# Selective attention and a gelu MLP on one core: narrow fills at the begin, none ahead of two attention steps, two items by halves, and DMA transposes moved between stores

## The chip, the cores and the metric

The kernel runs on one core of one Trainium2 chip. The metric is the device time of one execution in microseconds; before the change it is 306.07 us, the median of three runs (305.69 to 306.65).

## What is computed

There are 8 batches of 8 heads with 576 positions and 64 dimensions a head. Scores get a causal mask and a decay from the running sum of `s`, then a softmax; the result, with the heads side by side, is `x` with 4608 rows of 512. Two matrix products with an exact gelu between them follow.

```
scores = scale * np.matmul(q, k.transpose(0, 1, 3, 2))
bias = -(cum[:, :, :, None] - cum[:, :, None, :])          # cum: running sum of max(s, 0)
scores = np.where(causal, -1000000000.0, scores + np.minimum(bias, 0.0))
attn = softmax(scores)
x = (attn @ v) with heads side by side                     # 4608 x 512
out = gelu(x @ w_in) @ w_out                               # 512 -> 2048 -> 512
```

## The kernel before, in words

The work is cut in 9 chunks of 512 rows of `x`. While chunk `c` goes through the two products of the MLP, the attention of the next batch is computed between them, and the tensors of the batch after that are loaded. All of it is written out in order by hand (a manual schedule): each engine executes its instructions in the order of the program, and the eight PSUM banks are given out by name: three pairs of banks X, Y and Z and two single ones, M[0] and M[1]. `bank(slot, ...)` (L97) hands a slot on, and whoever writes it next waits until those who used it last are done.

Batch 0 has nothing in front of it, so its attention stands alone at the begin of the program, before the loop over the chunks:

- `fill` (L399) issues matrix products of ones whose result nobody reads. There are 28 of 192 columns at the begin, into M[1], then pairs of 512 columns at six places, one behind the first transposes and five between the later steps of batch 0.
- `tr_mm` and copies bring q and k of batch 0 into `qkT[0]` (q and k with positions along the free dimension). The first transposes wait for the load of `fq`.
- `sc_first(p, u, slot)` (L446) does the scores of one pair of heads in two parts: products of `off_bf` first, which put the mask into the bank (L453, L459), then those of q and k (L465), then one exponential on ScalarE (L471). The third and fourth pair (p = 2, 3) need the second half of the heads, whose k is copied last (L397 on VectorE).
- `av_first` (L542) sums the exponentials, weighted: the denominators into `d_ps`, the outputs into `oo`. It is done for the first 256 rows (part 0, banks M[0] and X) and for the next 256 (part 1, the second sums: banks M[1] and Y).
- `x_first` (L548) makes 1/denominator on ScalarE as exp(-ln) (L510, L511), and VectorE multiplies it into `xT` (L552), for one half of the heads at a time. So there are four ln, four exp and four products, in one order on each engine.
- `l1_first` (L578) is the hidden layer for items 0 and 1 of chunk 0, in quarters: first for the first 256 rows with the first half of the contraction (`k0 = 0`), items 0 and 1, then with the second half, then the same for the next 256 rows. Item 0 uses bank Z, item 1 bank X.

An item of the hidden layer is 256 of its 2048 columns: eight products of 512 columns in one pair of banks (`l1_item`, L595, products L605), then a gelu on ScalarE. Item `f2` uses the bank pair `f2 % 3` of the chunk's order, so item 7 takes over the bank of item 4. `layer1` (L798) issues items 2 to 7 one after another.

The batches from 2 on bring q and k in another way. POOL loads token rows (`load_tok`, L172) into buffers `tok`, one for each of the five stretches of 128 positions (the last has 64), and SP issues a DMA transpose for each into `qkT` (`transpose_tok`, L187, L190). SP's queue is in order. It also has the stores of chunk 0's four results (`l2_out`, L636) and loads of v for later batches (L204). Before the change the five transposes of batch 2 are issued at the begin of chunk 1, behind all stores of chunk 0, and POOL's loads of batch 3's tokens wait for them, as they use the same buffers. The scores of batch 2 (L436) come behind the hidden layer of chunk 1.

Of the kernel before, what the change touches and what calls it, by code (L numbers as in the profile page):

```python
# [19 lines left out]
def kernel(  # L20
# [22 lines left out]
    ST = 5  # L43
# [53 lines left out]
    def bank(slot, shape, dtype, name):  # L97

        return ps.tile(shape, dtype, tag=slot, bufs=1, name=name)
# [84 lines left out]
                    ),  # L184
                )

    def transpose_tok(b):  # L187
        for st in range(ST):
            n_st = 128 if st < ST - 1 else SL
            nc.sync.dma_start_transpose(  # L190
                out=qkT[b % 2][:, :, :, st * 128 : st * 128 + n_st].rearrange("d i p t -> d (i p) t"),
                in_=tok_of.pop((b, st))[:n_st].rearrange("t i c -> t (i c)"),
            )
# [19 lines left out]
    def absmax(b, ps_=range(NP)):  # L213

        for p in ps_:
            nc.vector.tensor_reduce(  # L216
                amx[:, b * NP + p], qkT[b % 2][:, :, p, :S], axis=AX, op=ALU.max, apply_absolute_value=True
            )

    def square_x(c):  # L220

        junk = work.tile([128, NP, NB], bf16, tag="junk", bufs=1, name="junk")
        nc.scalar.activation(  # L223
            junk, xT[:, :, c * NB % XW : c * NB % XW + NB], func=AF.Square, accum_out=sqx[:, c : c + 1]
        )

    def scale_v(b, sts, eng):

        t = raws[b, "v"].rearrange("p st h (d t) -> p st h t d", t=2)
        vb = vv[b % 2].rearrange("p st h (t d) -> p st h t d", t=2)  # L230
        for st0, st1 in sts:
            n_st = 128 if st1 < ST else SL
            for st in range(st0, st1):
                eng.tensor_tensor(  # L234
                    vb[:n_st, st], t[:n_st, st],
                    wb[:n_st, st, b * H : b * H + H].unsqueeze(2).unsqueeze(3).to_broadcast([n_st, H, 2, D // 2]),
                    op=MULT,
                )
# [154 lines left out]
    def copy(eng, out, in_):  # L393
        if eng is nc.scalar:
            eng.copy(out, in_)  # L395
        else:
            eng.tensor_copy(out, in_)  # L397

    def fill(t, n):  # L399

        cols = t.shape[1]
        for _ in range(n):
            nc.tensor.matmul(  # L403
                t, lhsT=xT[:, 3, 1024:1152], rhs=xT[:, 3, 1024 : 1024 + cols],
                start=True, stop=True, skip_group_check=True,
            )
# [21 lines left out]
    def sc_mm(b, p, slots, u0=0):  # L428
        if u0 == 0:
            P_of[b, p] = work.tile([128, 2, PW], bf16, tag="P", bufs=4, name="P")  # L430
        P = P_of[b, p]
        for u, slot in enumerate(slots, u0):
            s_ps = bank(slot, [128, 2, 512], fp32, "sc_ps")
            for jt, i0, n, off in UNITS[u]:
                for e in range(2):
                    nc.tensor.matmul(  # L436
                        s_ps[:, e, off : off + n],
                        lhsT=qkT[b % 2][e * 64 : e * 64 + 64, 1, p, jt * 128 : jt * 128 + 128],
                        rhs=qkT[b % 2][e * 64 : e * 64 + 64, 0, p, i0 : i0 + n],
                        start=True, stop=True,  # L440
                    )
            nc.scalar.activation(  # L442
                P[:, :, UO[u] : UO[u] + UW[u]], s_ps[:, :, : UW[u]], func=AF.Exp, scale=scale
            )
# [30 lines left out]
    def mask(b, p, eng):  # L475
        P = P_of[b, p]
        for u in range(NU):
            d = P[:, :, UO[u] : UO[u] + 512].rearrange("p e (g c) -> p e g c", c=256)[:, :, :, 0:128]
            eng.tensor_tensor(  # L479
                d, d, tri_bf.unsqueeze(1).unsqueeze(1).to_broadcast([128, 2, 2, 128]), op=MULT  # L480
            )
            if u == 1:
                d = P[:, :, UO[u] + 448 : UO[u] + 512]
                eng.tensor_tensor(
                    d, d, tri_bf[:, :64].unsqueeze(1).to_broadcast([128, 2, 64]), op=MULT
                )
# [55 lines left out]
    def av_first(c, qds, d_ps, oo, what=(None, 0, 1)):  # L542

        for qd in qds:
            for t in what:
                av_mm(0, qd, d_ps[:, qd] if t is None else oo[:, qd, t], t, PART[c])
# [48 lines left out]
    def l1_item(c, f2, k0=0, k1=None):  # L595
        k1 = KO if k1 is None else k1
        if f2 == 0 and k0 == 0:
            gT_of[c] = work.tile([128, FT, NB], fp16, tag="gT", bufs=1, name="gT")
        if k0 == 0:
            h_of[c, f2] = bank(order[c][f2 % 3], [128, 2, NB], fp32, "h_ps")  # L600
        h_ps = h_of[c, f2]
        for i in range(2):
            ft = f2 * 2 + i
            for ko in range(k0, k1):
                nc.tensor.matmul(  # L605
                    h_ps[:, i, :], lhsT=w_in_r[:, ko, ft * 128 : (ft + 1) * 128],
                    rhs=xT[:, ko, c * NB % XW : c * NB % XW + NB],
                    start=(ko == 0), stop=(ko == KO - 1),
                )
        if k1 == KO and f2 < FT // 2 - 1:  # L610
            nc.scalar.activation(gT_of[c][:, f2 * 2 : f2 * 2 + 2, :], h_ps, func=AF.Gelu)  # L611
        elif k1 == KO:
            for i in range(2):
                nc.scalar.activation(gT_of[c][:, f2 * 2 + i, :], h_ps[:, i], func=AF.Gelu)  # L614

    def l2_item(c, sub, f0=0, f1=FT, slot=None, eng=None, later=False):

        gT = gT_of[c]
        if f0 == 0:
            if slot is None:  # L620
                o_of[c, sub] = bank(M[sub % 2], [128, KO * 128], fp32, "o_ps")
            elif slot in M:
                o_of[c, sub] = bank(slot, [128, KO * 128], fp32, "o_ps")
            elif sub == 2:
                two = bank(slot, [128, 2, KO * 128], fp32, "o_ps")
                o_of[c, 2], o_of[c, 3] = two[:, 0], two[:, 1]
        o_ps = o_of[c, sub]
        for ft in range(f0, f1):
            nc.tensor.matmul(  # L629
                o_ps, lhsT=gT[:, ft, sub * 128 : (sub + 1) * 128],  # L630
                rhs=w_out_r[:, ft], start=(ft == 0), stop=(ft == FT - 1),
            )
        if f1 == FT and not later:
            l2_out(c, sub, eng)

    def l2_out(c, sub, eng=None):  # L636

        o_sb = work.tile([128, KO * 128], fp32, tag="osb", bufs=4, name="o_sb")
        copy(eng or nc.vector, o_sb, o_of[c, sub])
        r0 = c * NB + sub * 128  # L640
        nc.sync.dma_start(out=out[r0 : r0 + 128], in_=o_sb)
# [85 lines left out]
        load_w(1, i)  # L727
    both = (nc.vector, nc.vector)
    f_ps = bank(M[1], [128, 512], fp32, "fill")
    fill(f_ps[:, :192], 28)  # L730
    t_q = bank(X, [128, 2, 16, 64], bf16, "tr_ps")
    tr_mm(0, 0, 0, [t_q[:, pp] for pp in range(2)])
    nc.scalar.copy(
# [31 lines left out]
                t_k[:, pp, :FR, j * 32 : j * 32 + 32].rearrange("d r t -> d t r"),  # L765
            )
    f_ps = bank(M[1], [128, 512], fp32, "fill")
    fill(f_ps, 2)
    sc_first(2, 0, Y)
    fill(f_ps, 2)  # L770
    sc_first(3, 0, Z)
# [8 lines left out]
    oo0 = bank(X, [128, 2, 2, 256], fp32, "av_o")  # L780
    av_first(0, (0, 1), d0, None, (None,))
    av_first(0, (0, 1), None, oo0, (0, 1))
    fill(f_ps, 2)
    d1 = bank(M[1], [128, 2, 256], fp32, "av_d")
    av_first(1, (0, 1), d1, None, (None,))
    for qd in range(2):
# [11 lines left out]
    def layer1(c, after):  # L798

        for k0, k1 in ((0, KO - 2), (KO - 2, KO)):  # L800
            for f2 in range(2):
                if c > 0:
                    l1_item(c, f2, k0, k1)
            if c == 1 and k0 == 0:
                av_tails(1, M[0])
        after(1)
        for f2 in range(2, HT):
            l1_item(c, f2)
            after(f2)

    def products(c, order_):
# [4 lines left out]
    for c in range(NCH):  # L816
# [36 lines left out]
                    cert_4(M[1])  # L853

        if c == 1:
            transpose_tok(2)
            load_tok(3)
            absmax(1, [2, 3])
        elif c > 1:
            if nb < B:  # L860
                transpose_tok(nb)
                if nb + 1 < B:
                    load_v(nb + 1, nc.sync)
                    load_tok(nb + 1)
                scale_v(nb, STS[0:3], nc.vector)
            if c < B:
                square_x(c - 1)
                absmax(c, [0, 1])
        layer1(c, after)
        if c == 0:  # L870
            exp_set()
# [21 lines left out]
            l2_item(c, 2, 8, 12)  # L893
            l2_item(c, 3, 8, 12)
            sc_mm(1, 2, (z, x))
            l2_item(c, 0, 12, eng=nc.scalar)
            weight_sums(2)
            sc_mm(1, 3, (z,))
            l2_item(c, 1, 12, later=True)
            sc_mm(1, 3, (x,), 1)  # L900
            l2_out(c, 1, nc.scalar)
            scale_v(1, STS[0:2], nc.vector)
            mask(1, 2, nc.vector)
            scale_v(1, STS[2:5], nc.vector)
            l2_item(c, 2, 12, eng=nc.scalar)
            mask(1, 3, nc.vector)
            av_main(1, 0, M[0], z)
            l2_item(c, 3, 12)
# [263 lines left out]
```

## Time and profile before

| | |
|---|---|
| median of three runs | 306.07 us (305.69 to 306.65) |
| the profiled execution | 305.94 us |
| its span | 304.2 us |
| TensorE (PE) busy | 294.3 us, 97% |
| VectorE (DVE) busy | 226.1 us, 74% |
| ScalarE (ACT) busy | 225.2 us, 74% |
| mean granted TensorE clock | 0.997 |

A profile is one execution. Times are microseconds from the begin of the span. PE is TensorE's matrix products, PEld its weight loads, SPq and POOLq are the DMA queues of SP and POOL. In a row of the timeline the first number is the start, the second the time from there to the end of the last of its instructions, "xN" their count, and the bracket tells how long the engine sat idle before it and who ended that. "issue" is time in which the engine waited for nothing that the profile shows. PE's products are pipelined: the busy time of one is longer than the step to the next, so the pitch is read from starts. A few per cent of the product records are missing, so that counts can be one or two short. A row of a tile or line has the shortest, median and longest duration in ns, then the first and last start.

### The profile page before, as it was taken

The page shows a single profiled execution, that of the slowest core. Times are in us where ns is not written, and L with a number is a line of the kernel's source. Part 1 is how long each engine was busy: PE and PEld are TensorE (multiplying, and loading weights), DVE is VectorE, ACT ScalarE, POOL GpSimd, SP SyncE. Part 2 cuts the span into 40 slices and gives each one's busy share as a digit, 9 for nine tenths or more (in the row PEclk, how much of TensorE's full clock was granted, in tenths as well). Part 3 has the DMA queues.
Part 4 walks back from the last instruction along what each step waited for, and adds up shares of the span by engine and source line. Part 5 has one row for each costly group of instructions (what it writes and reads, how often), then busy time and mean ns, then how long its engine had stood idle before and what let it go on. Part 6 is the DMA issues. An engine that isn't in the chain of part 4 may idle for free.

```text
span 304.2 us, 8151 instructions
## 1 busy us (share of the span) xinstructions
PE 294.3 (97%) x3391; PEld 192.9 (63%) x3412; DVE 226.1 (74%) x511; ACT 225.2 (74%) x291; POOL 79.6 (26%) x103
## 2 busy tenths in 40 slices
PE   7989999999999999999999999999999999999993
PEld 6565444546884588458945785488547864884583
DVE  5758278976897878996997699768977874563751
ACT  3898757778797788878877987798788889575500
POOL 8883447446005500451027101720000000000000
PEclk9999999999999999999999999999999999999998
DMA  7999999999959993899399957997640220031004
GB/s 120 228 211 207 205 228 147 285 172 137 158 135 177 156 172 96 164 151 170 101 159 179 162 112 166 148 157 139 141 84 2 71 71 1 2 103 34 3 1 148
DMA packets 124748, 40.33 MB, mean 133 GB/s; under 512 B 109440, under 2 KB 122752, under 8 KB 124704
## 3 DMA queue, kind: packets, MB, share of 16 engines
q0 software_dynamic: 63280, 17.18, 57.1%
q1 hardware_dynamic: 61136, 22.31, 38.1%
q8 instruction: 28, 0.46, 0.7%
q10 hardware_dynamic: 288, 0.26, 0.3%
q14 instruction: 16, 0.13, 0.2%
HBM read 36.85 MB, written 9.44 MB: 152 GB/s over the span
## 4 chain that ended last, share of the span: by engine, by line
PE 89%; ACT 3%; DMA 3%; POOL 1%; issue 1%; DVE 1%; SPq 1%; ACTq 0%; POOLq 0%
PE h_ps L605 37%; PE pb L682 14%; PE pa L682 8%; PE pd L682 5%; PE pe L682 5%; PE sc_ps L436 4%; PE av_o L495 4%; PE o_ps L629 4%; DMA qkT<-tok 3%; PE av_d L495 1%; ACT P L442 1%; PE h_ps L587 1%; PE av_t L495 1%; PE tr_ps L388 1%; PE fill L403 1%
## 5 line engine op out<-in xcount | busy, mean ns | idle before, releaser
L605 PE MATMUL h_ps<-xT,w_in_r 128*128 128x512 bf16 x542 | 121.9, 379 | 1.1
L605 PEld LDWEIGHTS <-w_in_r 128*128 128x128 bf16 x560 | 54.5, 98 | 63.8 <-DVE xT L532 0.4
L611 ACT ACTIVATE gT<-h_ps 128x1024 f16<-128x1024 f32 x61 | 60.5, 1022 | 28.1 <-PE h_ps L605 28.1
L442 ACT ACTIVATE P<-sc_ps 128x1024 bf16<-128x1024 f32 x56 | 53.7, 1024 | 8.9 <-PE sc_ps L436 8.8
L682 PEld LDWEIGHTS <-gs 128*128 128x128 f16 x512 | 48.6, 98 | 7.5 <-issue 1.3
L178 POOL DMA_DIRECT2D tok<-in_q_dram x30 | 25.6, 852 | 104.2 <-DMA qkT<-tok 101.5
L664 DVE TENSOR_TENSOR gs<-gT 128x512 f16<-128x512 f16 (+1 forms) x80 | 29.1, 365 | 23.6 <-ACT gT L611 20.4
L216 DVE TENSOR_REDUCE amx<-qkT 128x2 f32<-128x1152 bf16 x32 | 42.2, 1343 | 0.1
L682 PEld LDWEIGHTS <-gT 128*128 128x128 f16 x384 | 37.0, 98 | 6.7 <-ACT gT L614 0.2
L682 PE MATMUL pa<-w_out_r,gT 128*128 128x256 f16 x256 | 31.6, 273 | 0.0
L682 PE MATMUL pb<-w_sums,gs 128*128 128x256 f16 x256 | 30.7, 273 | 0.0
L479 DVE TENSOR_TENSOR P<-P,tri_bf 128x512 bf16<-128x512 bf16 x56 | 22.3, 421 | 9.9 <-ACT P L442 9.8
L178 POOL DMA_DIRECT2D tok<-in_k_dram x30 | 25.8, 861 | 3.8 <-DMA w_out_r<-in_moe_w_out_dram 2.3
L234 DVE TENSOR_TENSOR vv<-raw_v,wb 128x512 bf16<-128x512 f32 (+1 forms) x40 | 25.4, 682 | 0.0
L532 DVE TENSOR_TENSOR xT<-av_o,ln 128x256 bf16<-128x256 f32 (+2 forms) x64 | 21.4, 385 | 3.4 <-ACT ln L511 2.5
L223 ACT ACTIVATE junk<-xT 128x2048 bf16<-128x2048 bf16 x9 | 17.1, 1898 | 0.1
L511 ACT ACTIVATE ln<-ln,lnb 128x256 f32<-128x256 f32 x32 | 16.3, 508 | 1.0
L436 PE MATMUL sc_ps<-qkT 64*128 64x256 bf16 x280 | 16.5, 250 | 0.5 <-DMA qkT<-tok 0.5
L664 DVE TENSOR_TENSOR gs<-gs,gT 128x512 f16<-128x512 f16 (+1 forms) x40 | 14.9, 372 | 1.4
L495 PE MATMUL av_o<-P,vv 128*32 128x256 bf16 (+1 forms) x528 | 15.3, 256 | 0.6 <-issue 0.6
L629 PE MATMUL o_ps<-w_out_r,gT 128*128 128x512 f16 x64 | 15.5, 380 | 0.2 <-ACT o_sb L395 0.2
L495 PEld LDWEIGHTS <-vv 128*32 128x32 bf16 x784 | 15.0, 96 | 1.1 <-issue 0.7
(131 smaller groups left out, 328.6 us busy)
## 6 DMA issues: line engine op xcount, KB each, us to landing
out_dram<-o_sb SPq DMA_DIRECT2D x35, 256.0 KB, 2.5
raw_v<-in_v_dram SPq DMA_DIRECT2D x20, 256.0 KB, 10.1
raw_v<-in_v_dram POOLq DMA_DIRECT2D x12, 256.0 KB, 6.7
tok<-in_q_dram POOLq DMA_DIRECT2D x24, 128.0 KB, 7.5
tok<-in_k_dram POOLq DMA_DIRECT2D x24, 128.0 KB, 8.1
w_out_r<-in_moe_w_out_dram POOLq DMA_DIRECT2D x4, 512.0 KB, 15.1
fq<-in_q_dram POOLq DMA_DIRECT2D x4, 288.0 KB, 10.1
fk<-in_k_dram POOLq DMA_DIRECT2D x4, 288.0 KB, 10.9
```

The source lines that it names most:

```text
L178: nc.gpsimd.dma_start(out=t[:n_st, i].rearrange("p (h d) -> p h d", d=D), in_=bass.AP(tensor=src.tensor, offset=src.offset + b * H * S * D ...
L216: nc.vector.tensor_reduce(amx[:, b * NP + p], qkT[b % 2][:, :, p, :S], axis=AX, op=ALU.max, apply_absolute_value=True)
L234: eng.tensor_tensor(vb[:n_st, st], t[:n_st, st], wb[:n_st, st, b * H : b * H + H].unsqueeze(2).unsqueeze(3).to_broadcast([n_st, H, 2, D // ...
L436: nc.tensor.matmul(s_ps[:, e, off : off + n], lhsT=qkT[b % 2][e * 64 : e * 64 + 64, 1, p, jt * 128 : jt * 128 + 128], rhs=qkT[b % 2][e * 6 ...
L442: nc.scalar.activation(P[:, :, UO[u] : UO[u] + UW[u]], s_ps[:, :, : UW[u]], func=AF.Exp, scale=scale)
L479: eng.tensor_tensor(d, d, tri_bf.unsqueeze(1).unsqueeze(1).to_broadcast([128, 2, 2, 128]), op=MULT)
L495: nc.tensor.matmul(o[g * 32 : g * 32 + 32, lo : lo + n], lhsT=(wb[:, jt, b * H + h : b * H + h + 1].to_broadcast([128, 32]) if t is None e ...
L605: nc.tensor.matmul(h_ps[:, i, :], lhsT=w_in_r[:, ko, ft * 128 : (ft + 1) * 128], rhs=xT[:, ko, c * NB % XW : c * NB % XW + NB], start=(ko ...
L611: nc.scalar.activation(gT_of[c][:, f2 * 2 : f2 * 2 + 2, :], h_ps, func=AF.Gelu)
L629: nc.tensor.matmul(o_ps, lhsT=gT[:, ft, sub * 128 : (sub + 1) * 128], rhs=w_out_r[:, ft], start=(ft == 0), stop=(ft == FT - 1),)
L664: nc.vector.tensor_tensor(*todo[i][:3], op=todo[i][3])
L682: nc.tensor.matmul(ps_[:, sub - at], lhsT=lhs[:, j, sub * 128 : sub * 128 + 128], rhs=rhs[:, j], start=not more and j == 0 and sub == subs ...
```

## The change

It has five parts: 70 fills of 80 columns at the begin instead of 28 of 192; no fills ahead of the third pair's scores; none ahead of the second sums; items 4 and 5 of chunk 0 in halves of the contraction (4, 5, then 4, 5); and batch 2's transposes issued in chunk 0, two behind the scores of batch 1's third pair, two behind the second store and one behind the third.

```diff
-    def transpose_tok(b):
-        for st in range(ST):
+    def transpose_tok(b, sts=range(ST)):
+        for st in sts:
...
     f_ps = bank(M[1], [128, 512], fp32, "fill")
-    fill(f_ps[:, :192], 28)
+    fill(f_ps[:, :80], 70)
...
     f_ps = bank(M[1], [128, 512], fp32, "fill")
-    fill(f_ps, 2)
     sc_first(2, 0, Y)
     fill(f_ps, 2)
     sc_first(3, 0, Z)
...
     av_first(0, (0, 1), d0, None, (None,))
     av_first(0, (0, 1), None, oo0, (0, 1))
-    fill(f_ps, 2)
     d1 = bank(M[1], [128, 2, 256], fp32, "av_d")
     av_first(1, (0, 1), d1, None, (None,))
...
         for f2 in range(2, HT):
-            l1_item(c, f2)
+            if c == 0 and f2 == 4:
+                for k0 in (0, 2):
+                    for i in (4, 5):
+                        l1_item(c, i, k0, k0 + 2)
+            elif c > 0 or f2 != 5:
+                l1_item(c, f2)
             after(f2)
...
         if c == 1:
-            transpose_tok(2)
             load_tok(3)
             absmax(1, [2, 3])
...
             sc_mm(1, 2, (z, x))
+            transpose_tok(2, (0, 1))
             l2_item(c, 0, 12, eng=nc.scalar)
...
             l2_out(c, 1, nc.scalar)
+            transpose_tok(2, (2, 3))
             scale_v(1, STS[0:2], nc.vector)
...
             l2_item(c, 2, 12, eng=nc.scalar)
+            transpose_tok(2, (4,))
             mask(1, 3, nc.vector)
```

On PE, between the outputs of part 0 (`av_o`) and the denominators of part 1 (`av_d`, the second sums), the difference reads as follows ("wb" are the weights of the sums, "PE" in a wait is PE's own progress):

```order
 L495 LDWEIGHTS vv_102
 L495 MATMUL av_o<-P,vv_102 32x128
-L403 LDWEIGHTS xT
-L403 MATMUL fill<-xT 128x512
...
 L495 LDWEIGHTS wb
 L495 MATMUL av_d<-P,wb 32x128 [waits PE_49]
```

The pair of fills is gone, and the first product of `av_d` still waits for the last fill into its bank M[1], which is now one ahead of the last scores.

On PE in the hidden layer's first quarter, at the first product of item 1 (bank X, in which the outputs of part 0 were):

```order
 L587 LDWEIGHTS w_in_r
 L587 MATMUL h_ps<-xT,w_in_r 128x256
-L587 LDWEIGHTS w_in_r
-L587 MATMUL h_ps<-xT,w_in_r 128x256 [waits DVE_49]
+L587 LDWEIGHTS w_in_r [waits DVE_49]
+L587 MATMUL h_ps<-xT,w_in_r 128x256 [waits PE_49]
 L587 LDWEIGHTS w_in_r
 L587 MATMUL h_ps<-xT,w_in_r 128x256
```

The place is the same: the item waits for VectorE's reads of bank X in both, and in the changed kernel for PE's own writes of it as well.

On SP, the stores of chunk 0 and the transposes of batch 2 before (the DMASW waits are for the tokens):

```order
L641 DMA out_dram<-o_sb 128x512 [waits Activation_49] x3
L641 DMA out_dram<-o_sb 128x512 [waits DVE_49]
L190 DMA_TRANSPOSE qkT_104<-tok_996 128x8x128 [waits DMASW5_49,DMASW4_49,PE_49]
L190 DMA_TRANSPOSE qkT_104<-tok_999 128x8x128 [waits DMASW7_49,DMASW6_49,PE_49]
L190 DMA_TRANSPOSE qkT_104<-tok_1002 128x8x128 [waits DMASW1_49,DMASW0_49,PE_49]
L190 DMA_TRANSPOSE qkT_104<-tok_1005 128x8x128 [waits DMASW3_49,DMAHW0_49,DMASW2_49,PE_49]
L190 DMA_TRANSPOSE qkT_104<-tok_1008 128x8x64 [waits DMASW5_49,DMAHW1_49,DMASW4_49,PE_49]
L204 DMA raw_v<-in_v_dram 128x8x64 [waits DMAHW2_49]
```

And in the changed kernel:

```order
L190 DMA_TRANSPOSE qkT_104<-tok_1034 128x8x128 [waits DMASW4_49,DVE_49,DMASW5_49,PE_49,Activation_49]
L190 DMA_TRANSPOSE qkT_104<-tok_1037 128x8x128 [waits DMASW7_49,DMASW6_49,PE_49]
L641 DMA out_dram<-o_sb 128x512 [waits Activation_49] x2
L190 DMA_TRANSPOSE qkT_104<-tok_1040 128x8x128 [waits DMASW1_49,DMASW0_49,PE_49]
L190 DMA_TRANSPOSE qkT_104<-tok_1043 128x8x128 [waits DMASW3_49,DMASW2_49,PE_49]
L641 DMA out_dram<-o_sb 128x512 [waits Activation_49]
L190 DMA_TRANSPOSE qkT_104<-tok_1046 128x8x64 [waits DMASW5_49,DMAHW0_49,DMASW4_49,PE_49]
L641 DMA out_dram<-o_sb 128x512 [waits DMAHW1_49,DVE_49]
L204 DMA raw_v<-in_v_dram 128x8x64 [waits DMAHW2_49]
```

All five transposes are ahead of the last store, two of them ahead of every store.

## The prediction

> **What bounds the kernel now.** I read the page first, then the chain of waits, then the timeline of the four places that the change touches. The page:
>
> ```profile
> span 304.2 us, 8151 instructions
> PE 294.3 (97%) x3391; PEld 192.9 (63%) x3412; DVE 226.1 (74%) x511; ACT 225.2 (74%) x291; POOL 79.6 (26%) x103
> PEclk9999999999999999999999999999999999999998
> PE 89%; ACT 3%; DMA 3%; POOL 1%; issue 1%; DVE 1%; SPq 1%; ACTq 0%; POOLq 0%
> ```
>
> TensorE is busy 97% of the span, and 89% of the chain that ended last is its own work. So the only time to be had is where TensorE waits, or works on fills. PE's list of waits is short. Behind the begin its two longest rows are these: a gap that no semaphore explains, and a wait for a DMA.
>
> ```profile
> PE av_o L495 <- issue: 0.6, 1, 0.6
> PE sc_ps L436 <- DMA qkT<-tok: 0.5, 1, 0.5
> ```
>
> The profiled execution took 305.94 us, its span 304.2 us; the other 1.7 us lies outside the span and stays. The median of the runs, 306.07, is 0.13 us above the profiled one.
>
> **The change, part by part. The fills at the begin.** Mean durations hide the pitch, so I take it from the first and last start. Below are the fills in two windows, the next work on PE and the wait of its weight loads, and two later products, 64 and 256 columns wide, which both load weights of their own.
>
> ```profile
> L403 PE MATMUL fill<-xT x24: 343/368/368, 1.5 to 5.1; 128*128 128x192 bf16 x24
> L403 PE MATMUL fill<-xT x5: 246/273/367, 5.1 to 5.6; 128*128 128x192 bf16 x5
> 6.37 0.48 PE L388 MATMUL tr_ps<-ident_bf,fq 64*64 64x64 bf16 x36 [0.48 <-DVE cum L153]
> PEld L388 <- DMA fq<-in_q_dram: 0.7, 1, 0.7
> 10.47 0.19 PE L459 MATMUL sc_ps<-off_bf,ident_bf 128*128 128x64 bf16 x1
> 10.50 0.27 PE L453 MATMUL sc_ps<-off_bf,ident_bf 128*128 128x256 bf16 x1
> ```
>
> 24 fills start between 1.5 and 5.1 us, so 23 pitches take 3.6 us: 157 ns for 192 columns, 0.82 ns a column. The last ones are quicker (246 instead of 368 ns), so the array goes up to its full rate about 3.9 us after the first fill. Seventy fills of 80 columns are 5600 columns instead of 5376: at 0.82 ns a column 66 ns each, 59 of them by 5.4 us, and the other 11 at half of that take 0.4 us: they end at about 5.8 us, and at 6.1 us if the rate never rises (70 x 66 ns = 4.6 us). The transposes behind them start at 6.37 us, and that start was set by the landing of fq, so this part costs 0. The bound from above is that a narrow fill can't hide its weight load: 131 ns, the mean of the loads in this stretch, times 70 is 9.2 us, which ends at 10.7 us and costs 4.3 us.
>
> ```profile
> L403 PEld LDWEIGHTS <-xT 128*128 128x128 bf16 x40 | 4.7, 131 | 2.4 <-DVE xT L120 1.5 <-issue 0.6
> ```
>
> I take 0, because the product of 64 columns gave way to the next one, with a new load of 128x128 weights, after 30 ns (10.47 to 10.50); twice that at half rate is 60 ns and fits below 66. [...]
>
> **The fills ahead of the third pair.** PE, then the copies that its products wait for:
>
> ```profile
> 12.38 0.39 PE L403 MATMUL fill<-xT 128*128 128x512 bf16 x1
> 12.83 0.38 PE L453 MATMUL sc_ps<-off_bf,ident_bf 128*128 128x256 bf16 x2
> 13.14 0.39 PE L465 MATMUL sc_ps<-qkT 64*128 64x256 bf16 x4
> 12.52 1.19 DVE L397 COPY qkT<-tr_ps 128x288 bf16<-128x288 bf16 x3 [0.62 <-PE tr_ps L388]
> ```
>
> Without two fills (12.38 to 12.83) the mask products could start 0.43 us sooner, but the score products need the first of the copies, three of which take 1.19 us: done at 12.9 to 13.0. So they start at about 13.02 instead of 13.14: 0.12 us, not 0.43. PE's next steps, and with them ScalarE's four exponentials, keep this 0.12.
>
> **The fills ahead of the second sums.** PE, then ScalarE and VectorE in the same stretch:
>
> ```profile
> 17.17 0.83 PE L495 MATMUL av_o<-P,vv 128*32 128x256 bf16 x32
> 18.16 0.38 PE L403 MATMUL fill<-xT 128*128 128x512 bf16 x1 [0.16 <-issue]
> 18.59 0.62 PE L495 MATMUL av_d<-P,wb 128*32 128x128 bf16 x24
> 19.03 0.66 PE L495 MATMUL av_o<-P,vv 128*32 128x128 bf16 x25
> 20.25 0.62 PE L495 MATMUL av_o<-P,vv 128*32 128x128 bf16 x23 [0.56 <-issue]
> 20.80 1.16 PE L587 MATMUL h_ps<-xT,w_in_r 128*128 128x256 bf16 x9
> 17.87 0.38 ACT L510 ACTIVATE ln<-av_d 128x256 f32<-128x256 f32 x1
> 18.82 1.50 DVE L552 TENSOR_TENSOR xT<-av_o,ln 128x512 bf16<-128x512 f32 x2 [2.35 <-ACT ln L511]
> 19.91 0.51 ACT L511 ACTIVATE ln<-ln,lnb 128x256 f32<-128x256 f32 x1
> ```
>
> The second sums waited for the fills' own end, as they use their bank. They can now follow av_o, which ends at 18.00: 0.59 us sooner. With the 0.12 from above they end at 20.87 - 0.71 = 20.16 even if the gap of 0.56 us (at 19.7) stays whole, and at 19.6 without it. I take the gap as going: between a load and its product, with no semaphore, it looks like PE waiting for its next instructions. 76 more instructions ahead of it move it to where PE was 76 instructions earlier, and what is needed next then has been asked for during the scores, with their pauses. [...]
>
> What is late next is the hidden layer's second item. Its bank X is the one that the first sums' results were in, so it waits for both xT products of VectorE (18.82 + 1.50 = 20.32), which hang on ScalarE's chain of ln and exp, not on PE. That chain follows the exponentials without a pause and gains only their 0.12: done at 20.20, the item starts at 20.25. Before, it started behind four products of the first: 20.80 + 4 x 0.11 = 21.24. The gain here is 0.99 us, not the 1.27 that PE alone would give (0.59 + 0.56 + 0.12). The later quarters don't wait: the third xT product is done at 19.91 + 0.51 - 0.12 + 0.7 = 21.0 and wanted at 20.25 + 12 x 0.11 = 21.6.
>
> **Items 4 and 5 by halves.**
>
> ```profile
> 24.31 10.52 PE L605 MATMUL h_ps<-xT,w_in_r 128*128 128x512 bf16 x47
> L247 POOL DMA_DIRECT2D w_in_r<-in_moe_w_in_dram x1: 707/707/707, 15.1 to 15.1; - x1
> DMA to landing us min/median/max: 11.5/11.5/11.5
> ```
>
> Same 16 products, other order: 0. The gelu of item 4 comes about 0.86 us later, but item 7, which takes over its bank, comes three items later. The last weights of these items landed at 15.1 + 11.5 = 26.6 us, as the rows of their DMA say; item 4 starts two items behind 24.31 - 0.99, with 8 products of 0.22 us in an item, at about 26.8 us, so neither order waits for them.
>
> **The transposes between stores.** The token loads of batch 2 (the landing is for q and k together), SP's queue, a piece of the chain, the scores of batch 2 and, for comparison, those of batch 3, which don't wait:
>
> ```profile
> L178 POOL DMA_DIRECT2D tok<-in_k_dram x5: 681/873/888, 40.8 to 50.9; - x5
> DMA to landing us min/median/max: 5.2/7.5/12.0
> 57.87 10.02 SPq L190 DMA_TRANSPOSE qkT<-tok  x5
> 66.31 7.73 DMA qkT<-tok
> 73.10 0.50 PE L436 MATMUL sc_ps<-qkT 64*128 64x256 bf16 x6
> 74.08 0.51 PE L436 MATMUL sc_ps<-qkT 64*128 64x192 bf16 x8 [0.47 <-DMA qkT<-tok]
> 74.51 0.72 PE L682 MATMUL pb<-w_sums,gs 128*128 128x256 f16 x5
> 105.11 0.83 PE L436 MATMUL sc_ps<-qkT 64*128 64x256 bf16 x14
> 105.87 1.38 PE L682 MATMUL pb<-w_sums,gs 128*128 128x256 f16 x11
> 67.63 1.89 DVE L234 TENSOR_TENSOR vv<-raw_v,wb 128x512 bf16<-128x512 f32 x3
> ```
>
> From scores to products it is 1.41 us in batch 2 and 0.76 in batch 3: the wait costs 0.65. The five transposes take 16.2 us from first issue to last landing (57.87 to 74.04). The first tokens, issued at 40.8 at the latest, land within 12.0 us, so the transposes can start by 52.8 and land by 69.0; the scores come at 73.10 - 0.99 = 72.1. So 0.65 goes; from 0 to 0.65 is the bound. Behind the waiting transposes on SP are only the stores of chunk 0, whose four buffers are next filled by chunk 1's results, behind the scores of batch 2, and the loads of v for batch 3; POOL's loads of batch 3's tokens, which wait for the transposes, start sooner.
>
> **Sum:** 0.99 + 0.65 = 1.64 us: 305.94 - 1.64 = 304.3 for the profiled run, 304.4 for the median.
>
> **Rivals.** (1) The gap stays, or falls elsewhere on the path. PE then ends the sums at 20.16, the second item starts at 20.6, and the gain there is 0.64 instead of 0.99: 304.8. (2) The transposes land as late as now, since stores and the loads of v go through the same DMA engines: only 0.99 is left, 305.1. (3) Slower: narrow fills bound by their weight loads. It decides once a fill takes more than 70 ns, as 6.37 is then passed; at 131 ns it gives 304.4 + 4.3 = 308.7. For it: no row shows narrow fills in a stream. (4) Fills gone, the array's rate falls back as at the begin: a slow stretch as long as the first, 3.9 us, would lose half of it, 1.9 us: 306.3. Against: right after the pause of 0.56 us the products of 256 columns came every 0.11 us (nine in 1.16), 0.43 ns a column, which is the quick rate. (5) Transposes ahead of batch 2's v delay its scaling on VectorE, and with it the sums behind it that TensorE multiplies. It decides if v lands after 67.63 - 0.99 = 66.6; each us beyond costs at most one, so 3 us would give 307.4.
>
> **Chances.** Forecast 0.70, (1) 0.12, (2) 0.06, (3) 0.05, (4) 0.04, (5) 0.03. What a measurement can tell from no change is 0.3%, 0.9 us, that is 305.15. Forecast, (1) and half of (2) are faster by more, less a little for the spread of the runs (305.69 to 306.65): 0.83; the other half of (2), (4) and that spread 0.11; (3) and (5) 0.06. The range goes from the whole 1.27 + 0.65 less half a spread (306.07 - 1.92 - 0.5 = 303.6) up to (2) with 0.3 of spread: 305.4.
>
> **What would show it.** Right: transposes of q still at 6.4 us; L465 of the third pair near 13.0; the first L587 near 19.5 with a short wait for xT, the 32 of them done 1 us sooner; no DMA wait in L436; and pb of the next chunk at 104.2 instead of 105.87. Wrong: L388 starting after 6.5, an issue gap of half a us elsewhere in PE, or L436 still waiting for qkT.

## The result and the profile after

The changed kernel takes 312.81 us, the median of six runs (311.44 to 314.25), beside 305.52 us for the kernel before (304.67 to 306.65): a ratio of 1.0239, 95% interval 1.0201 to 1.0278. It is slower by 7.3 us, where 1.6 us less was forecast. The profiled run took 313.99 us, its span is 311.9 us, 7.8 more than before.

Three lines of the page of the changed kernel:

```profile
span 311.9 us, 8248 instructions
PEclk9999999999599999999999999999999999999998
PE 89%; DMA 5%; ACT 2%; issue 1%; POOL 0%; DVE 0%; ACTq 0%; POOLq 0%
```

TensorE (PE) is still nearly the whole chain, but there is more DMA in it, and one of the forty slices has half the clock. Two rows of PE's list of waits (in total, times, longest):

```profile
PE sc_ps L436 <- DMA qkT<-tok: 5.1, 3, 2.2
PE av_d L495 <- issue: 0.4, 1, 0.4
```

And its timeline, first at the begin, then around the scores of batch 2:

```profile
1.47 4.71 PE L403 MATMUL fill<-xT 128*128 128x80 bf16 x70 [1.47 <-DVE xT L120]
6.64 0.48 PE L388 MATMUL tr_ps<-ident_bf,fq 64*64 64x64 bf16 x36 [0.45 <-DMA fq<-in_q_dram]
18.92 0.44 PE L495 MATMUL av_d<-P,wb 128*32 128x128 bf16 x13 [0.44 <-issue]
20.17 3.71 PE L587 MATMUL h_ps<-xT,w_in_r 128*128 128x256 bf16 x32
23.72 10.52 PE L605 MATMUL h_ps<-xT,w_in_r 128*128 128x512 bf16 x48
...
72.74 0.28 PE L436 MATMUL sc_ps<-qkT 64*128 64x256 bf16 x2
74.19 0.29 PE L436 MATMUL sc_ps<-qkT 64*128 64x256 bf16 x2 [1.16 <-DMA qkT<-tok]
76.25 0.28 PE L436 MATMUL sc_ps<-qkT 64*128 64x256 bf16 x2 [1.78 <-DMA qkT<-tok]
78.74 0.82 PE L436 MATMUL sc_ps<-qkT 64*128 64x192 bf16 x8 [2.21 <-DMA qkT<-tok]
79.49 3.60 PE L682 MATMUL pb<-w_sums,gs 128*128 128x256 f16 x16
82.88 1.78 PE L682 MATMUL pa<-w_out_r,gT 128*128 128x256 f16 x8
85.36 1.92 PE L682 MATMUL pb<-w_sums,gs 128*128 128x256 f16 x16
87.12 1.04 PE L682 MATMUL pa<-w_out_r,gT 128*128 128x256 f16 x8
```

The begin did bring time: the hidden layer starts at 20.17 instead of 20.80, and L605 at 23.72 instead of 24.31. Nearly all is lost at the scores of batch 2. Each of three transposes is waited for (1.16 + 1.78 + 2.21 = 5.15 us), and behind that sixteen products `pb` take 3.60 us and eight of `pa` 1.78, against 1.92 and 1.04 six us later. The clock explains the second part; windows of 2 us:

```profile
76.00:78.00 2.00, 0.28 (x2) 0.11 (x3) 0.00 (x0) 0.00 (x0) 1.35 (x3) 0.89 1.80 176
78.00:80.00 2.00, 1.26 (x11) 0.73 (x11) 0.00 (x0) 0.83 (x1) 1.59 (x3) 0.50 1.44 224
84.00:86.00 2.00, 2.00 (x26) 1.45 (x25) 1.34 (x3) 0.97 (x2) 0.00 (x0) 0.90 1.77 157
```

The third number from the end of a row is the granted clock. It is a half from 77.6 to 84.4 us. The sum along PE, from starts in both traces: at the first scores of batch 2 the changed kernel is 0.36 us ahead (72.74 against 73.10), at `pb` 4.98 behind (79.49 against 74.51), at the sums behind it (`av_d`) 7.36 behind (90.48 against 83.13), at the end 7.8. So 8.1 us are lost from the scores on: 5.3 up to `pb`, most of it the waits (5.15, where the kernel before waited 0.47; the last scores, from 78.74 on, also run at half the clock), 2.4 behind that by the clock, 0.4 in small pieces, 0.27 of it one gap at 93 us. The two rows of `av_d`, of the kernel before and of the changed one:

```profile
83.13 0.57 PE L495 MATMUL av_d<-P,wb 128*32 128x256 bf16 x16
90.48 0.57 PE L495 MATMUL av_d<-P,wb 128*32 128x256 bf16 x16
```

SP's queue in the timeline shows where the transposes were held up:

```profile
49.85 5.83 SPq L190 DMA_TRANSPOSE qkT<-tok  x2
57.92 11.32 SPq L190 DMA_TRANSPOSE qkT<-tok  x2
70.03 1.96 SPq L190 DMA_TRANSPOSE qkT<-tok  x1
```

The rows of their line (ns to issue one: shortest, median, longest; then us from issue to landing), first of the kernel before, then of the changed one:

```profile
L190 SPq DMA_TRANSPOSE qkT<-tok x5: 1250/1582/3787, 57.9 to 66.3; - x5
DMA to landing us min/median/max: 4.1/5.8/7.7
L190 SPq DMA_TRANSPOSE qkT<-tok x5: 1960/3050/5704, 49.8 to 70.0; - x5
DMA to landing us min/median/max: 8.7/12.7/16.2
```

The first was issued 8 us earlier than before (49.85 instead of 57.87), the last 3.7 us later (70.03 instead of 66.31). From issue to landing it is 12.7 us in the median instead of 5.8, and SP is kept by an issue for 3.1 us in the median instead of 1.6. The DMA engines did not move more meanwhile, but less. Their packets from 54 to 56 us, of the kernel before and of the changed one:

```profile
DMA packets 595, 0.57 MB, mean 284 GB/s; under 512 B 427, under 2 KB 427, under 8 KB 595
DMA packets 603, 0.11 MB, mean 56 GB/s; under 512 B 603, under 2 KB 603, under 8 KB 603
```

With POOL's loads and the transposes under way together, 56 GB/s came through, where it had been 284. Part of this is what was moved: before, 168 of the packets were of 2 KB and more, of `v` and the stores; in the changed kernel all are small ones, of tokens and transposes. That small packets alone go faster is shown in the last section.

### The profile page after: what moved, and what is told of

The parts are those of the page before. It is cut to its first block, busy times and chain, and to the rows that moved or that the text cites. A ratio compares the mean times of both kernels' runs of the same rounds, so it can differ in the third digit from the quotient of the medians.

```text
span 311.9 us, 8248 instructions
## 1 busy us (share of the span) xinstructions
PE 298.3 (96%) x3450; PEld 194.4 (62%) x3450; DVE 226.3 (73%) x511; ACT 225.5 (72%) x291; POOL 79.6 (26%) x103
## 4 chain that ended last, share of the span: by engine, by line
PE 89%; DMA 5%; ACT 2%; issue 1%; POOL 0%; DVE 0%; ACTq 0%; POOLq 0%
PE h_ps L605 39%; PE pb L682 15%; PE pa L682 8%; PE pd L682 5%; PE pe L682 4%; PE sc_ps L436 4%; PE o_ps L629 3%; PE av_o L495 3%; DMA qkT<-tok 3%; DMA fq<-in_q_dram 2%; PE av_d L495 1%; ACT P L442 1%; PE av_t L495 1%; PE h_ps L587 1%; PE tr_ps L388 1%; PE two L495 1%
## 5 line engine op out<-in xcount | busy, mean ns | idle before, releaser
L605 PE MATMUL h_ps<-xT,w_in_r 128*128 128x512 bf16 x560 | 123.0, 379 | 0.1
L605 PEld LDWEIGHTS <-w_in_r 128*128 128x128 bf16 x560 | 54.5, 98 | 63.8 <-DVE xT L532 0.4
L682 PEld LDWEIGHTS <-gs 128*128 128x128 f16 x512 | 49.4, 99 | 8.4 <-issue 1.5
L682 PE MATMUL pa<-w_out_r,gT 128*128 128x256 f16 x256 | 32.4, 277 | 0.0
L682 PE MATMUL pb<-w_sums,gs 128*128 128x256 f16 x256 | 32.4, 282 | 0.0
L436 PEld LDWEIGHTS <-qkT 64*128 64x128 bf16 x280 | 10.9, 95 | 12.4 <-issue 9.7
L682 PE MATMUL pb<-w_sums,gT 128*128 128x256 f16 x128 | 15.3, 273 | 0.0
```

Of the source, the lines that this page charges most:

```text
L436: nc.tensor.matmul(s_ps[:, e, off : off + n], lhsT=qkT[b % 2][e * 64 : e * 64 + 64, 1, p, jt * 128 : jt * 128 + 128], rhs=qkT[b % 2][e * 6 ...
L605: nc.tensor.matmul(h_ps[:, i, :], lhsT=w_in_r[:, ko, ft * 128 : (ft + 1) * 128], rhs=xT[:, ko, c * NB % XW : c * NB % XW + NB], start=(ko ...
L682: nc.tensor.matmul(ps_[:, sub - at], lhsT=lhs[:, j, sub * 128 : sub * 128 + 128], rhs=rhs[:, j], start=not more and j == 0 and sub == subs ...
```

## Experiments

The transposes and the fills apart from each other, and theories to tell between. For the transposes, M: loads by POOL and transposes that are under way together hold each other up; Q: it is the alternation with stores in SP's one queue; later T: the loads of tokens alone hold the transposes up. For gaps on PE that no semaphore explains, F: instruction fetch.

**begin_only.** The transposes back at the begin of chunk 1, all else as changed.

```diff
         if c == 1:
+            transpose_tok(2)
             load_tok(3)
...
-            transpose_tok(2, (0, 1))
...
-            transpose_tok(2, (2, 3))
...
-            transpose_tok(2, (4,))
```

> The changed kernel with the five transposes of batch 2 back at the begin of chunk 1, all other parts kept. Both theories below blame the moved transposes, so both expect the loss of 7.3 us to be gone: the scores of batch 2 wait for qkT once, about 0.5 us, as before. The begin parts gave 0.36 us by 72.7 us in the profile of the changed kernel (the products pa of chunk 1 start at 70.90 instead of 71.26), so 305.2, and 304.9 if the later landing of q at the begin (6.6 instead of 6.3 us) was chance. If the time is still over 308, some other part of the change costs, and both theories are wrong.

306.96 us, ratio 1.0046 (1.0030 to 1.0062). No score product waits for a transpose any more, and at `pb` of chunk 1 the kernel is 0.71 us ahead of before (73.80 against 74.51). But it is slower than before; both theories had missed something. PE's timeline, 11 us later:

```profile
84.84 0.34 PE L495 MATMUL av_t<-P,vv 128*32 128x64 bf16 x18
86.77 0.29 PE L495 MATMUL av_t<-P,vv 128*32 128x64 bf16 x14 [1.59 <-issue]
```

In the middle of 32 equal products PE stands for 1.59 us, and nothing of the kernel is waited for.

**transposes_only.** The kernel before with the transposes moved, nothing else.

```diff
         if c == 1:
-            transpose_tok(2)
...
+            transpose_tok(2, (0, 1))
...
+            transpose_tok(2, (2, 3))
...
+            transpose_tok(2, (4,))
```

> The kernel before with only the transposes moved. Both theories: three waits of the scores of batch 2 for qkT, together about 5 us, and a slower granted clock behind them worth about 2.4 us: 305.5 + 7.5 = 313. If it is under 308, the loss needs another part of the change beside the transposes.

309.35 us, ratio 1.0114 (1.0069 to 1.0158), from 306.98 to 311.59. The wait is there (2.3 us in the profile: 0.3 and 2.0), the clock did not fall in this run. The moved transposes alone cost 1.6 to 6.3 us (over the 305.33 of before on this chip), differently in each run; 313 was too much.

**v_behind.** Batch 2's `v` by SP behind the last transpose.

```diff
             load_tok(2)
-            load_v(2)
...
             transpose_tok(2, (4,))
+            load_v(2, nc.sync)
```

> The changed kernel with the five loads of batch 2's v issued by SP behind the last transpose, instead of by POOL from 51 us on. Theory M (mixing): transposes and POOL's loads of v hold each other up when both are under way; without the loads each transpose takes 1 to 2 us, the five land by 64 us, no score product waits for qkT, SP's issues of a transpose take about 1.3 us instead of up to 5.7, and the time is 304.5 to 305.5, with up to 2 us more if v now comes late for VectorE (its scaling was due at 67.6). Theory Q (queue): what holds the transposes up is that they alternate with stores in SP's queue; nothing of that is changed, the issues still take 3 to 6 us, and the time stays at 311 to 313.

The rows of the transposes' line:

```profile
L190 SPq DMA_TRANSPOSE qkT<-tok x5: 1282/1356/3097, 49.8 to 61.3; - x5
DMA to landing us min/median/max: 6.2/7.3/8.0
```

A row of PE's waits:

```profile
PE pb L682 <- DVE gs L664: 6.2, 1, 6.2
```

And the first scaling of this `v` in VectorE's timeline:

```profile
70.14 0.69 DVE L234 TENSOR_TENSOR vv<-raw_v,wb 128x512 bf16<-128x512 f32 x1 [4.80 <-DMA raw_v<-in_v_dram]
```

The transposes are better: the last lands at 68.6 us instead of 78.7, and no score product waits. They are still 6.2 to 8.0 us under way, and later than M's 64: POOL still loads beside them, tokens of batch 2 until 57 us and of batch 3 from 58 us. But the time is 314.45 (1.0304, 1.0270 to 1.0338): `v` is now late for VectorE (its first scaling at 70.14, where the kernel before has it at 65.90), the sums `gs` stand behind it in VectorE's queue, PE waits 6.2 us for them, and the clock is at half for 6.83 us from 78.8 on. M is borne out for the transposes, Q is not; M's 2 us for a late `v` was three times too little.

**one_block.** All five transposes at the first place, ahead of the stores.

```diff
-            transpose_tok(2, (0, 1))
+            transpose_tok(2)
...
-            transpose_tok(2, (2, 3))
...
-            transpose_tok(2, (4,))
```

> The changed kernel with all five transposes at the first of the three places, ahead of the stores of items 1 to 3, so that SP's queue no longer alternates. Theory M: they still run beside POOL's loads of tokens and of v (51 to 63 us before), so they still land late, the last behind 70 us, and the time is 309 to 314; the stores behind them come late too. Theory Q: the transposes go at 1.3 us each and land by 62 us, no score product waits, 304.5 to 305.5.

The rows of the transposes' line:

```profile
L190 SPq DMA_TRANSPOSE qkT<-tok x5: 1212/2946/6919, 50.0 to 65.2; - x5
DMA to landing us min/median/max: 7.7/10.4/14.5
```

And PE's timeline behind the next sums:

```profile
88.05 0.29 PE L495 MATMUL av_t<-P,vv 128*32 128x64 bf16 x14 [2.62 <-issue]
88.28 2.62 PE L682 MATMUL pd<-w_sums,gs 128*128 128x256 f16 x16
```

310.51 us (1.0181, 1.0142 to 1.0220). No store stands between, and still an issue takes up to 6.9 us and the last lands at 73.6: Q falls, M had said this. The scores wait only 0.5 us for it. The time is lost at `av_t` again, 2.62 us, and by the clock behind that (16 products `pd` in 2.62 us instead of 1.92).

**aligned and narrow_only.** These gaps led to counting PE's instructions. In the program's order of PE the gap in the kernel before (at 19.7 us) stands ahead of instruction 694, a product `av_o`; that of the changed kernel (at 18.5) ahead of 694 too, which is 76 instructions earlier work, `av_d`; that of begin_only and of one_block ahead of 2484, seven times 256 farther to within 2. The traces' own count says the same: these gaps stand behind the 351st and the 1246th weight load in each of these kernels, 895 loads apart, and to each load there is one product. A stretch of 256 instructions of PE that ends at one of these places is called a block here. `aligned` is begin_only with the old numbers:

```diff
-    fill(f_ps[:, :80], 70)
+    fill(f_ps[:, :176], 32)
```

> The kernel begin_only with 32 fills of 176 columns instead of 70 of 80 (5632 columns instead of 5600), so that every instruction of PE behind the begin has the number that it has in the kernel before. Theory F (instruction fetch): PE's gaps without a semaphore lie at instruction 695 in the kernel before and in the changed one, at 2485 in begin_only and one_block, which is 7 x 256 farther; they belong to the number, not to the work. Then the gap of 1.6 us in av_t at 85 us is gone, one of about 0.6 us comes back at 19 us behind the 24th to 26th product of av_o, the hidden layer starts 0.3 to 0.6 us earlier than in the kernel before, and the time is 304.6 to 305.3. Rival D: the gap at 85 us comes from what the DMA queues carry there and stays: 306.5 to 307.

Four rows of PE's timeline in it:

```profile
14.90 0.38 PE L403 MATMUL fill<-xT 128*128 128x512 bf16 x1 [1.04 <-issue]
19.47 0.66 PE L495 MATMUL av_o<-P,vv 128*32 128x128 bf16 x25
21.37 0.62 PE L495 MATMUL av_o<-P,vv 128*32 128x128 bf16 x23 [1.24 <-issue]
86.03 0.46 PE L495 MATMUL av_t<-P,vv 128*32 128x64 bf16 x32
```

The gap at `av_t` is gone, the one ahead of 694 is back, and a further one stands at 438, 256 earlier. 305.11 us beside 305.54 (ratio 0.9983, 0.9958 to 1.0008): not told apart from before. So all of the change but the moved transposes and the shifted numbers brings no gain that these runs can show. In the profiled run, one of the slower ones (306.53), the hidden layer starts later than before, not earlier as F's forecast had it. `narrow_only` is the opposite test, the kernel before with the 70 narrow fills:

```diff
-    fill(f_ps[:, :192], 28)
+    fill(f_ps[:, :80], 70)
```

> The kernel before with 70 fills of 80 columns at the begin instead of 28 of 192, nothing else changed: 84 instructions more on PE. Theory F: the end of a block of 256 lies in the first half of av_t's products at 84 us (those are issued fastest, about 66 in a us), so a gap of 1 to 2.6 us comes there; the one at 19 us goes or shrinks; 306.0 to 307.5. Rival D, and the prediction's own view of the fills: nothing changes, 305.3.

PE's timeline:

```profile
85.30 0.28 PE L495 MATMUL av_t<-P,vv 128*32 128x64 bf16 x14
87.48 0.32 PE L495 MATMUL av_t<-P,vv 128*32 128x64 bf16 x18 [1.90 <-issue]
```

307.26 us (1.0048, 1.0027 to 1.0069). Behind the fills nothing but the numbers of the instructions has changed, and that costs 1.9 us at `av_t`, in this run with 3.41 us at half the clock behind it; the gap at 19.7 is gone in return (the hidden layer starts at 20.19 instead of 20.80). The profiled run is the slowest of thirteen (310.33); by the ratio the runs lose 1.5 us.

**shift40.** begin_only with other fills once more.

```diff
-    fill(f_ps[:, :80], 70)
+    fill(f_ps[:, :108], 52)
```

> The kernel begin_only with 52 fills of 108 columns instead of 70 of 80 (5616 columns instead of 5600): 36 instructions of PE fewer behind the begin. Theory F: the gap without a semaphore stays at the same number, 2486, and therefore moves to other work: av_t ends at 2466 here, so the gap comes behind the ninth or tenth product of pd (w_sums, gs), not in av_t; the block in front of it still holds nearly only quick products, so it is again 1 to 2.5 us; 306 to 308. At the begin it comes at 694 behind the eighth product of the second av_o. Rival W: the gap belongs to av_t's work and stays in av_t, or goes.

PE's timeline:

```profile
84.90 0.61 PE L682 MATMUL pd<-w_sums,gs 128*128 128x256 f16 x4
86.44 1.47 PE L682 MATMUL pd<-w_sums,gs 128*128 128x256 f16 x12 [0.93 <-issue]
```

306.67 us (1.0034, 1.0017 to 1.0052). `av_t` runs through, and the gap stands in `pd`, ahead of its fifth product, which is 2484 once more (I had miscounted it as the ninth or tenth), and takes 0.93 us, a little less than forecast. At 694 there is none this time, where F had one. W falls.

**v_ahead and v_ahead_between.** `v` of batch 2 ahead of its tokens, with the old numbers; the transposes in one block, or between the stores.

```diff
-            load_tok(2)
-            load_v(2)
+            load_v(2)
+            load_tok(2)
```

> The kernel aligned with batch 2's loads of v issued by POOL ahead of the token loads instead of behind them; the transposes in one block at the begin of chunk 1. Theory M: the transposes start at about 57.5 with no load of v under way, land within 1 to 2 us each, the last by 68, and no score product waits for qkT; v is early as well: 0.4 to 0.6 us less than aligned, 304.2 to 304.8. If mixing with v is not what holds them up, they land between 70 and 74 as in the kernel before, and the time is that of aligned.

> The kernel changed as asked (transposes between the stores), with the fills of aligned and batch 2's loads of v ahead of the token loads. Theory M: without loads of v beside them the moved transposes do no harm: the last lands by 70, no score product waits for more than 0.5 us, 304.2 to 305.3. Theory Q (stores between transposes in one queue): the issues on SP still take 3 to 6 us, the last transpose lands behind 74, 308 to 312. If the token loads alone hold the transposes up (theory T), the first two land late, behind 60, and the last behind 72: 306 to 310.

306.02 us (1.0011, 0.9991 to 1.0031) and 306.79 (1.0046, 1.0019 to 1.0073). In v_ahead no `v` is under way, and the transposes are late nevertheless; the rows of their line, then the one of PE's waits:

```profile
L190 SPq DMA_TRANSPOSE qkT<-tok x5: 1246/1836/4607, 56.8 to 68.3; - x5
DMA to landing us min/median/max: 5.4/6.2/9.5
```

```profile
PE sc_ps L436 <- DMA qkT<-tok: 1.5, 1, 1.5
```

Now the tokens, issued 5 to 9 us later, are what lands beside them, up to 68 us. So M with `v` alone falls. Between the stores (v_ahead_between) the first two land at 63.3 and 65.5 us, the last at 74.3, and a score product waits 0.5 us for it, though stores alternate with them: that is T's forecast in times of landing and in the total, not M's (the last by 70) and not Q's (308 to 312). T's "alone" does not hold, since v_behind gained by taking `v` away; so M was widened to any load by POOL, of tokens or of `v`.

**quiet.** The kernel before, with POOL held back until the transposes are done.

```diff
-            load_tok(3)
+            load_tok(3, (4,))
+            load_v(2)
+            load_tok(3, range(4))
...
             load_tok(2)
-            load_v(2)
```

> The kernel before with POOL silent while the transposes run: of batch 3's token loads the last stretch comes first, so that POOL waits for the last transpose, then batch 2's v, then the other tokens. Theory M, widened after v_ahead (any load by POOL, of tokens or of v, that is under way holds the transposes up, and they it): the transposes, issued from 57.9 us on behind the stores, land 1.0 to 1.6 us apart, the last by 67 (74.0 before), each issue on SP takes 1.2 to 1.6 us, and no score product waits for qkT. Theory B (the transposes themselves are slow, or SP's queue is): 2 us or more each, the last behind 70. The time is of no use, since v comes some 10 us late for VectorE: 308 to 316.

The rows of the transposes' line:

```profile
L190 SPq DMA_TRANSPOSE qkT<-tok x5: 1193/1261/2065, 57.0 to 63.4; - x5
DMA to landing us min/median/max: 2.9/3.4/4.0
```

The five land from 61.0 to 66.2 us, 0.9 to 1.5 us apart, and no score product waits. That is widened M; B (the transposes themselves, or SP's queue, are slow) falls. The time is 315.18 us in one run, for the late `v`, as expected.

**filled_wait.** The changed kernel with products of no use in the three waits.

```diff
             for jt, i0, n, off in UNITS[u]:
+                for _ in range((0, 5, 8, 10, 0)[jt] if pad is not None else 0):
+                    nc.tensor.matmul(pad, lhsT=w_in_r[:, 0, :128], rhs=w_in_r[:, 0, :512], ...)
```

> The changed kernel with 5, 8 and 10 products of 512 columns, whose result nobody reads, ahead of the second, third and fourth pair of the first score products of batch 2, where PE waits for the transposes. If the slower granted clock behind these waits comes from the pauses, the clock stays at 1.0 there, sixteen products pb take 1.9 us again instead of 3.6, and eight of pa 1.04 instead of 1.78: 2.4 us less than the changed kernel, some 310.5. If it comes from something else, pb still takes over 3 us, 312 to 314.

PE's timeline behind the waits (the lines are five farther here):

```profile
79.68 1.92 PE L687 MATMUL pb<-w_sums,gs 128*128 128x256 f16 x16
81.44 1.04 PE L687 MATMUL pa<-w_out_r,gT 128*128 128x256 f16 x8
```

The last scores come at 79.25, no sooner than in the changed kernel (78.74), but the clock stays whole: `pb` takes 1.92 us, `pa` 1.04, and the kernel 311.1 us in one run (span 309.3 instead of 311.9). That time by itself says little, as the changed kernel's own runs go down to 311.44; the products and the granted clock, 1.00 from 76 to 84 us here, say that it was the pauses that had let the clock fall.

## Why the prediction was wrong

**The transposes: the step that failed.** "The five transposes take 16.2 us from first issue to last landing [...] so the transposes can start by 52.8 and land by 69.0." This carried a duration along to another place as if it belonged to the transposes. By themselves they take 9.2 us from first issue to last landing (quiet, 57.0 to 66.2); the 16.2 already held waiting for POOL's loads, and at the new place there were more of these: tokens until 59 us, `v` until 69. There they took 28.9 us (49.85 to 78.70). Rival (2) named the right neighbours, other transfers, but stopped at "as late as now" and 0.65 us; it was 4.7 us later than now. In times: with the transposes back at their place (begin_only) 5.9 of the 7.3 us are gone, and moved by themselves (transposes_only) they cost 4.0 us in the median. That the transfers are slow because they share engines is not shown; that they are slow together is.

**The cost of waiting.** The prediction priced a wait at its length. Three pauses, 5.15 us in 6, put PE back by 5.3 us and then by 2.4 more, since the clock fell to a half for 6.8 us. Rival (4) thought of this only for the fills taken out; there it was rightly held unlikely: behind the places without fills the products of 256 columns still came every 0.11 us (32 of them in the 3.55 us from 20.17 to 23.72), the quick rate.

**The instruction gap: half right.** "76 more instructions ahead of it move it to where PE was 76 instructions earlier" is what happened: still ahead of 694. That "what is needed next then has been asked for during the scores" is not: it stood for 0.44 us there, so rival (1) came true for the begin. What the step left out is the work farther on: with the same 76 instructions number 2484, seven blocks behind 694, falls among the quick products at 85 us, and PE stands there. It is worth 1.6 us in begin_only and 1.9 in narrow_only; in the changed kernel itself, where that stretch came 8 us later and the fetch (a packet of 16 KB, last section) landed 1.4 us behind its start instead of 2.8 (91.87 against 90.48, 85.22 against 82.42), only 0.3 us. Pricing the new fills at zero was right for their own stretch alone.

**The begin, in sizes.** 70 fills came every 65 ns (66 forecast), so weight loads don't bound them and rival (3) falls. (Its 131 ns was the mean over all forty fills up to 25 us, not of the first 28 alone; nothing hangs on it.) From the transposes of k to the third pair's scores it is 1.06 us instead of 1.17: the forecast 0.12. The second sums follow `av_o` without a pause, as forecast. L605 is 0.59 us earlier, not 0.99; rival (1) said 0.64. That this comes so near is in part luck: between runs this moves more than the change. With the same instructions up to there, L605 starts at 25.43 in aligned, 23.27 in v_ahead and 24.56 in v_ahead_between, with the landings of q and k and the length of the gaps.

**The halves** cost nothing: the products from item 2 on take 10.52 us in both.

**Late `v`**, rival (5), did not come in the changed kernel, but v_behind and quiet show that its mechanism was right, and that 6 to 7 us of waiting for `gs` hang on it. Its limit of 66.6 us was read from the wrong row: 67.63 is where three middle stretches of `v` are scaled. The first is scaled at 65.90:

```profile
65.90 0.69 DVE L234 TENSOR_TENSOR vv<-raw_v,wb 128x512 bf16<-128x512 f32 x1
```

## What to carry to other kernels

A transfer's time in a profile holds that of its neighbourhood (the five transposes took 9.2 us by themselves and 28.9 beside POOL's loads): before moving one, look at what is in flight at the new place, and give a DMA transpose a stretch in which no other queue loads, as far as the schedule allows it; here `v` was then late. Count instructions as well as time: a few dozen more at the begin changed what work stood at 694 and at 2484 on PE, and where 2484 fell among quick small products PE stood there for 0.3 to 2.6 us. Price a wait of TensorE of several us with the slower clock that may come behind it: here waits of 5.15 us cost 2.4 us more by that.

## What the runs showed of the hardware

**Transposes beside loads.** By themselves the transposes land 0.9 to 1.5 us apart, 2.9 to 4.0 us after their issue; beside POOL's loads they are 4 to 16 us under way, and the loads are late too (the last of `v` from 63.5 to 68.8 us). Packets in 2 us, of the transposes alone (quiet, 60 to 62 us) and of the token loads alone (the kernel before, 50 to 52):

```profile
DMA packets 1656, 0.41 MB, mean 204 GB/s; under 512 B 1656, under 2 KB 1656, under 8 KB 1656
DMA packets 2246, 0.30 MB, mean 150 GB/s; under 512 B 2245, under 2 KB 2245, under 8 KB 2245
```

Together, in the changed kernel from 54 to 56 us, it was 603 packets and 56 GB/s, though all of them are small ones (under 512 B) of the same two kinds. For part of that time the engines stand idle: of forty slices of these 2 us, seventeen show them busy for three tenths or less. Why is not settled; the profile doesn't show which engine waits for which.

**Instruction fetch.** Every one of these gaps ends 1.4 to 1.7 us after a packet of 16 KB has landed on the queue that the profile calls instruction (q8); such a packet is a fetch here:

| kernel | fetch landed | PE goes on | ahead of instruction | work |
|---|---|---|---|---|
| before | 18.77 | 20.25 | 694 | `av_o` |
| changed | 17.55 | 18.92 | 694 | `av_d` |
| changed | 91.87 | 93.35 | 2484 | `av_t` |
| aligned | 13.42 | 14.90 | 436 or 438 | fill |
| aligned | 19.73 | 21.37 | 694 | `av_o` |
| begin_only | 85.22 | 86.77 | 2484 | `av_t` |
| one_block | 86.33 | 88.05 | 2484 | `av_t` |
| narrow_only | 86.11 | 87.48 | 2484 | `av_t` |
| shift40 | 85.08 | 86.44 | 2484 | `pd` |
| v_ahead | 87.64 | 89.15 | 2484 | `pe` |

The 256 instructions ahead of 2484, quick products and their weight loads, take 2.8 us (82.4 to 85.2 in begin_only). The packet itself takes 0.9 us in the changed kernel, begin_only and one_block; what differs is how long after the start of that stretch its fetch begins: 0.5 us in the changed kernel (90.98 against 90.48), 1.9 in begin_only (84.34 against 82.42), 2.8 in one_block (85.45 against 82.67), and the gaps are 0.3, 1.59 and 2.62 us. Even with the earliest of these three fetches 2.87 us pass from the start of the stretch to the product at 2484 (90.48 to 93.35), and with the later ones, by 1.4 and 2.3 us, the gap is longer by about as much (1.3 and 2.3). In v_behind, where the fetch begins 1.3 us ahead of the stretch (89.59 against 90.91), the same products run through. Most such packets have no such gap behind them: the kernel before has 28 and the changed one 29, and the only pauses of over 0.3 us on PE that no semaphore explains are those at 694 (0.56 and 0.44 us). What makes a fetch begin late is not shown. That it is full DMA queues is argued from where the gaps are: in later chunks, which have the same products and fewer loads, the pauses in the sums are 0.3 us at most (at 219 us in v_behind).

**How long the clock stayed at a half.** It was a half for 6.83 us in the changed kernel and in v_behind, for 3.41 behind the gap of 2.62 us in one_block and that of 1.90 in narrow_only, for 10.24 in quiet: two, one and three times 3.41 (at the end of a run, where the profile cuts it off, it is other lengths). A pause of 2.05 us in transposes_only brought no fall, nor did that of 1.59 in begin_only (a mean granted clock of 1.0 in both). So a pause of 1.90 us was followed by a fall in one run and one of 2.05 us by none in another. Why is not shown.
